# One ring of three two-bank PSUM buffers for the first layer and the attention

## The chip, the cores and the metric

The kernel runs on one core of a Trainium2 chip. The metric is device time in microseconds (us) of one launch; lower is better. The core has five engines that run their own instruction queues in order: TensorE (PE in the profile; its weight loads are listed apart as PEld), VectorE (DVE), ScalarE (ACT), GpSimd (POOL) and SyncE (SP), which here issues every DMA. Matmuls write into PSUM, of which this kernel uses eight banks of 512 fp32 columns in 128 partitions; DVE and ACT read it from there.

## The reference, cut to what matters

All data are float32 (the two weight matrices come as float64). Agent attention runs first, over two batches of 12480 tokens, 49 agents and 128 channels; its output goes through one dense layer pair with an ELU between.

```python
scale = 1.0 / np.sqrt(q.shape[-1])
def sm(a, b):
    s = scale * (a @ b.transpose(0, 2, 1))
    s = s - s.max(-1, keepdims=True)
    e = np.exp(s)
    return e / (e.sum(-1, keepdims=True) + 1e-09)
agent_v = sm(agents, k) @ v            # per batch: 49 x 128
x = (sm(q, agents) @ agent_v).reshape(B * S, D)
h = x @ w_in                           # 24960 x 2048
g = np.where(h > 0.0, h, np.exp(np.minimum(h, 0.0)) - 1.0)
out = g @ w_out                        # 24960 x 128
```

The kernel never forms x. It multiplies agent_v by w_in once per batch (49 x 2048, called A), and h is the query softmax times A.

## The kernel before, in words

**Tiling.** A block is 960 tokens (8 groups of 120); there are 13 blocks a batch, 26 in all. A block is worked in two halves of 480 tokens, each half in 8 steps, and a step covers 256 of the 2048 hidden columns. So the main loop has 26 x 2 x 8 = 416 steps, and a period of 16 steps is one block. High and low parts of fp32 numbers are kept apart (hi and lo, px and py for the two parts and two orders of the softmax rows), which is why a step has several matmuls for one product.

**A step s** is, in the order in which the loop at the end of the function writes it: `p1(s)`, six matmuls into a two-bank tile h (line 407); `p2(s - 4)`, eight matmuls of an earlier step into the output banks o0 and o1 (line 437), and after the eighth step of a half two DVE operations that add these into ob (lines 440, 441) and its DMA; `elu(s)`, Relu and Exp on ACT (413, 414) and the DVE operation that makes g (416); `split(s)`, the DVE cast hi (422) and the POOL subtraction lo (line 194, called through `rest`); and then whatever `at(s, ...)` has put into the table `pre` for this step. Nothing reorders this: the order is written by hand, each engine runs its own part of it in order, and semaphores follow from the tiles that are written and read.

**PSUM.** Pool ps_h has two h tiles of two banks each, used in turn; ps_o has o0 and o1; ps_a has two single banks, at0 and at1, that `attn_bank` hands out and `attn_free` takes back. An h tile is free again when g of its step has been computed.

**Attention work in the table.** Let EDGE be 3. For query block j the table holds, from step s0 = 16 (j - 1) + 3 on: scores of 960 tokens (`q_scores`, 8 matmuls, line 146), the maximum and its subtraction one step later (`q_max` 303, `q_sub` 314), `q_exp` (320), `q_sum` (323), `q_rz` (328, 331), `q_mul` (335), `q_hi` (189) and `q_lo` (194), and at s0 + 8 and s0 + 9 the two halves of `q_tr`: four transposes each (361), a copy into px (362), and two DMAs that make py by swapping px's row groups (365, 366). The scores' bank is held from `q_scores` to the last `q_lo`: the exponentials are kept in it. Batch 1's keys are scored in 13 rounds, two a period, in steps 8 to 104 (`k_round`, then `k_out` a step later: an ACT copy, line 154, and DVE maxima, lines 160 and 164); then four small calls spread the maximum (`k_max_*`). From step 116 on each round's scores are shifted (`e_sub`, 198), exponentiated (`e_exp`, 201) and multiplied with v (`ev1_pe`, line 207, four matmuls and two steps later four more). All 104 of these matmuls add up in one bank, which is held for the whole stretch; `ev1_out` copies it. Then `av_pe`, `av_out` and four times `A_pe`, `A_hi`, `A_lo` make A of batch 1.

**Before the loop** batch 0's keys and values are worked, and the weights are converted from float64 (lines 97 to 110), which goes on into the first steps of the loop. Two tiles of the h ring, `two` and `hk`, serve here too.

Of the kernel before, what the change touches and what calls it, by code (L numbers as in the profile page):

```python
# [22 lines left out]
def tile_agent_attention_moe(  # L23
# [34 lines left out]
    v_p = ctx.enter_context(tc.tile_pool(name="v", bufs=5))  # L58
    sm_p = ctx.enter_context(tc.tile_pool(name="sm", bufs=2))
    wc_p = ctx.enter_context(tc.tile_pool(name="wc", bufs=2))  # L60
    ps_h = ctx.enter_context(tc.tile_pool(name="ps_h", bufs=2, space=bass.MemoryType.PSUM))
    ps_o = ctx.enter_context(tc.tile_pool(name="ps_o", bufs=1, space=bass.MemoryType.PSUM))
    ps_a = ctx.enter_context(tc.tile_pool(name="ps_a", bufs=1, space=bass.MemoryType.PSUM))

    ag_sb = const.tile([C, B, NA], F32)
    ident = const.tile([128, 128], F32)
# [61 lines left out]
        nc.sync.dma_start(out=t, in_=vx[b, :, r * R:(r + 1) * R, :])  # L128
        v_t[b, r] = t

    idle = [0, 1]
    held = {}

    def attn_bank(dt=F32):
        i = idle.pop(0)
        ps = ps_a.tile([128, 512], dt, tag=f"at{i}", name=f"at{i}")
        held[id(ps)] = i
        return ps

    def attn_free(ps):  # L140
        if id(ps) in held:
            idle.append(held.pop(id(ps)))

    def scores_pe(ps, src, b, lo, hi):
        for j in range(lo, hi):
            nc.tensor.matmul(out=ps[:TP, j * NA:(j + 1) * NA], lhsT=src[:, j * TP:(j + 1) * TP], rhs=ag_sb[:, b, :], start=True, stop=True)  # L146
# [58 lines left out]
    def ev_pe(ps, b, r, lo, hi, rs):  # L205
        for j in range(lo, hi):
            nc.tensor.matmul(out=ps, lhsT=s_all[:, r, j:j + 2, :].rearrange("p t a -> p (t a)"), rhs=v_t[b, r][:, j, :], start=(r == rs[0] and j == 0), stop=(r == rs[-1] and j == R - 1))  # L207
        if hi == R:
            v_t.pop((b, r))
# [20 lines left out]
        else:  # L230
            nc.vector.scalar_tensor_tensor(out=av["sv"], in0=ps, scalar=f, in1=av["sv"], op0=ALU.mult, op1=ALU.add)

    def ev1_pe(r, lo, hi):
        if r == 0 and lo == 0:
            ev_ps[0] = attn_bank()
        ev_pe(ev_ps[0][:2 * NA, 0:VW], 1, r, lo, hi, range(NR))

    def ev1_out():
        ps = ev_ps.pop(0)
        attn_free(ps)  # L240
        av["sv"] = sm_p.tile([NA, VW], F32, tag="sv", name="sv")
        nc.vector.tensor_copy(out=av["sv"], in_=ps[:NA, 0:VW])

    def av_pe():
        ps = attn_bank()
# [57 lines left out]
        nc.vector.tensor_reduce(out=mx, in_=v, axis=AX.X, op=ALU.max)  # L303
        q_st["mx"] = mx

    def q_sub(keep=True):
        ps = q_st.pop("ps")
        v = ps[:TP, 0:R * NA].rearrange("p (t a) -> p t a", a=NA)
        if keep:
            e, q_st["z"], q_st["bank"] = v, ps[:TP, 400:400 + R], ps  # L310
        else:
            e = sm_p.tile([TP, R, NA], F32, tag="qe", name="qe", bufs=1)
            q_st["z"] = sm_p.tile([TP, R], F32, tag="z", name="z")
        nc.vector.tensor_tensor(out=e, in0=v, in1=q_st["mx"].unsqueeze(2).to_broadcast([TP, R, NA]), op=ALU.subtract)
        if not keep:
            attn_free(ps)
        q_st["e"] = e

    def q_exp():
        nc.scalar.activation(out=q_st["e"], in_=q_st["e"], func=ACTF.Exp, scale=scale)  # L320

    def q_sum():
        nc.vector.tensor_reduce(out=q_st["z"], in_=q_st["e"], axis=AX.X, op=ALU.add)

    def q_rz(half):
        z = q_st["z"]
        if half == 0:
            nc.vector.tensor_scalar(out=z, in0=z, scalar1=1e-9, scalar2=None, op0=ALU.add)
        else:
            q_st["z"] = sm_p.tile([TP, R], F32, tag="z", name="z")  # L330
            nc.vector.reciprocal(out=q_st["z"], in_=z)

    def q_mul(eng):
        e = q_st["e"]
        eng.tensor_tensor(out=e, in0=e, in1=q_st["z"].unsqueeze(2).to_broadcast([TP, R, NA]), op=ALU.mult)
# [4 lines left out]
    def q_hi(eng):  # L340
        for h, t in enumerate(halves(pp_hi)):
            cast_hi(eng, t, q_st["e"][:, h * (R // 2):(h + 1) * (R // 2), :])

    def q_lo(eng, lo=0, hi=R):
        for x in range(lo, hi, R // 2):
            h = x // (R // 2)
            rest(eng, halves(pp_lo)[h], q_st["e"][:, x:x + R // 2, :], halves(pp_hi)[h])
        if hi == R:
            attn_free(q_st.pop("bank", None))

    def q_tr(j, part):

        if part == 0:
            p_t[j] = []
        src = (pp_hi, pp_lo)[part]
        x = sm_p.tile([NA2, T], F32R, tag=f"px{part}", name=f"px{part}")
        y = sm_p.tile([NA2, T], F32R, tag=f"py{part}", name=f"py{part}")
        p_t[j].append((x, y))
        ps = attn_bank(F32R)
        for i in range(R // 2):  # L360
            nc.tensor.transpose(ps[:NA2, i * TP:(i + 1) * TP], src[:, i, :], ident_r[:TP, :TP])  # L361
        nc.vector.tensor_copy(out=x, in_=ps[:NA2, 0:T])
        attn_free(ps)
        a, b = [slice(r, r + NA) for r in ROWS]
        nc.sync.dma_start(out=y[a].bitcast(F32), in_=x[b].bitcast(F32))
        nc.sync.dma_start(out=y[b].bitcast(F32), in_=x[a].bitcast(F32))
# [31 lines left out]

    def p1(s):
        j, half, c = at_step(s)  # L400
        h = ps_h.tile([128, 2, 512], F32, tag="h", name="h")
        ah, al = A[j // NG, c]
        hi, lo = p_t[j]
        for i, (a, p) in enumerate([(ah, hi), (ah, lo), (al, hi)]):
            for u, r in enumerate(ROWS):
                x = slice(r, r + NA)
                nc.tensor.matmul(out=h[:, u, 0:T], lhsT=a[x, :], rhs=p[u ^ half][x, :], start=i == 0, stop=i == 2)  # L407
        h_t[s] = h[:, :, 0:T]
# [40 lines left out]
    def at(s, fn, *a):  # L449
        pre.setdefault(s, []).append((fn, a))  # L450

    with tc.manual_schedule():
        with tc.tile_pool(name="pro", bufs=5) as pro:
# [33 lines left out]
            two = ps_h.tile([128, 2, 512], F32, tag="h", name="h")  # L487
# [60 lines left out]
            def spread():  # L548
# [25 lines left out]
                ("e11", lambda: q_tr(0, 0), lambda: q_tr(0, 1)),  # L574
# [36 lines left out]
        for j in range(1, B * NG):  # L611
            s0 = (j - 1) * NM + EDGE
            if j + 1 < B * NG:
                at(s0 + 1, load_q, j + 1)
            if j > 1:
                at(s0, q_scores, j, 0, R)
                at(s0 + 1, q_max)
                at(s0 + 1, q_sub)
            at(s0 + 2, q_exp)
            at(s0 + 3, q_sum)  # L620
            at(s0 + 3, q_rz, 0)
            at(s0 + 4, q_rz, 1)
            at(s0 + 4, q_mul, dve)
            at(s0 + 5, q_hi, act)
            at(s0 + 6, q_lo, dve, 0, 4)
            at(s0 + 7, q_lo, dve, 4, 8)
            at(s0 + 8, q_tr, j, 0)
            at(s0 + 9, q_tr, j, 1)
        ks = {}
# [12 lines left out]
        KM = (3, 4, 6, 7)
        at(k_end + KM[0], lambda: k_max_t(mx_st["run"], attn_bank()))
        at(k_end + KM[1], k_max_d, 0)
        at(k_end + KM[2], lambda: k_max_b(attn_bank()))
        at(k_end + KM[3], k_max_c)
# [61 lines left out]
```

## Time and profile before

| | us |
|---|---|
| median of 3 runs | 1227.63 |
| lowest and highest | 1218.49, 1231.73 |
| the profiled execution | 1230.22 |
| its span, first to last instruction | 1228.4 |
| start of the first step of the loop | 70.4 |

Mean granted TensorE clock over the span: 0.966. A line of the timeline has the start in us from the span's start, the duration in us, the engine, the line, the operation, what it writes and reads, shapes and a count; in brackets the idle time of the engine before it and what ended that. A line of a group has busy time, the mean duration of one in ns, and the idle time before it. A line of a stretch has from:to, its length, then busy time of each engine with the number of instructions, the granted clock, the share of the DMA engines and GB/s.

### The profile page before, as it was taken

The page shows a single profiled execution, that of the slowest core. Times are in us where ns is not written, and L with a number is a line of the kernel's source. Part 1 is how long each engine was busy: PE and PEld are TensorE (multiplying, and loading weights), DVE is VectorE, ACT ScalarE, POOL GpSimd, SP SyncE. Part 2 cuts the span into 40 slices and gives each one's busy share as a digit, 9 for nine tenths or more (in the row PEclk, how much of TensorE's full clock was granted, in tenths as well). Part 3 has the DMA queues.
Part 4 walks back from the last instruction along what each step waited for, and adds up shares of the span by engine and source line. Part 5 has one row for each costly group of instructions (what it writes and reads, how often), then busy time and mean ns, then how long its engine had stood idle before and what let it go on. Part 6 is the DMA issues. An engine that isn't in the chain of part 4 may idle for free.

```text
span 1228.4 us, 21453 instructions
## 1 busy us (share of the span) xinstructions
PE 1166.6 (95%) x8184; PEld 815.3 (66%) x8184; DVE 883.5 (72%) x1353; ACT 881.2 (72%) x998; POOL 523.6 (43%) x443
## 2 busy tenths in 40 slices
PE   9877999999999999999999999999999999999998
PEld 9844666666666666667666566666666666666676
DVE  5564576676777676776767777778777777778775
ACT  3344676676777676776777778887878788787886
POOL 0123343344444343443444444544445444544454
PEclk9877899899999899999999999999999999999999
DMA  9940112112112113113001001101110101100000
GB/s 288 244 135 1 37 49 70 37 41 77 38 42 61 54 46 89 54 41 94 21 25 45 22 27 43 46 21 38 34 45 21 45 26 45 32 35 33 21 30 17
DMA packets 25709, 66.63 MB, mean 54 GB/s; under 512 B 3054, under 2 KB 14806, under 8 KB 25606
## 3 DMA queue, kind: packets, MB, share of 16 engines
q1 hardware_dynamic: 25606, 65.26, 17.4%
q8 instruction: 64, 1.05, 0.4%
q14 instruction: 39, 0.32, 0.1%
HBM read 42.68 MB, written 12.78 MB: 45 GB/s over the span
## 4 chain that ended last, share of the span: by engine, by line
PE 61%; DVE 20%; ACT 12%; issue 3%; DMA 3%; POOL 0%; DVEq 0%; SPq 0%; ACTq 0%; POOLq 0%
PE o L437 30%; PE h L407 18%; DVE g L416 11%; PE at L146 6%; ACT e L414 5%; ACT e L413 5%; PE at L207 2%; DVE hi L422 2%; PE at L361 2%; DMA v<-in_vx_dram 1%; PE h L207 1%; DVE mx L303 1%; DVE ob L441 1%; DVE ob L440 1%; PE at L262 1%
## 5 line engine op out<-in xcount | busy, mean ns | idle before, releaser
L194 POOL TENSOR_TENSOR lo<-g,hi 128x480 fp32r<-128x480 f32 x416 | 506.9, 1219 | 641.1 <-DVE hi L422 543.0
L416 DVE SCALAR_TENSOR_TENSOR g<-e,h 128x960 f32<-128x960 f32 x416 | 478.7, 1151 | 226.2 <-ACT e L414 215.6
L413 ACT ACTIVATE e<-h 128x960 f32<-128x960 f32 x416 | 403.0, 969 | 243.3 <-PE h L407 195.4
L414 ACT ACTIVATE e<-e 128x960 f32<-128x960 f32 x416 | 418.7, 1007 | 13.1
L437 PE MATMUL o<-g,w_f 64*128 64x480 f32 x1664 | 422.3, 574 | 0.0
L437 PE MATMUL o<-lo,w_hi 64*128 64x480 f32 x832 | 330.4, 766 | 0.0
L407 PE MATMUL h<-px,ahi 49*128 49x480 f32 x832 | 275.7, 411 | 19.6 <-DVE g L416 13.9
L407 PE MATMUL h<-py,ahi 49*128 49x480 f32 x832 | 275.7, 411 | 10.6 <-DVE g L416 7.2
L422 DVE CAST hi<-g 128x480 fp32r<-128x480 f32 x416 | 171.4, 412 | 57.6 <-PE o L437 3.8
L407 PEld LDWEIGHTS h<-px,ahi 49*128 49x128 f32 x832 | 135.2, 189 | 85.3 <-DVE g L416 56.5
L437 PE MATMUL o<-hi,w_lo 64*128 64x480 f32 x832 | 177.8, 388 | 13.9 <-POOL w_lo L194 8.2
L437 PEld LDWEIGHTS o<-g,w_f 64*128 64x128 f32 x1664 | 168.6, 189 | 24.0
L407 PEld LDWEIGHTS h<-py,ahi 49*128 49x128 f32 x832 | 135.1, 189 | 70.4 <-DVE g L416 48.9
L437 PE MATMUL o<-hi,w_hi 64*128 64x480 f32 x832 | 172.5, 385 | 0.0
L407 PE MATMUL h<-px,alo 49*128 49x480 f32 x416 | 159.6, 384 | 2.9 <-DVE alo L284 2.9
L407 PE MATMUL h<-py,alo 49*128 49x480 f32 x416 | 159.4, 383 | 0.1
L437 PEld LDWEIGHTS o<-lo,w_hi 64*128 64x128 f32 x832 | 89.0, 190 | 83.4 <-issue 79.7
L437 PEld LDWEIGHTS o<-hi,w_lo 64*128 64x128 f32 x832 | 87.0, 187 | 39.8 <-DVE ob L441 11.8
L437 PEld LDWEIGHTS o<-hi,w_hi 64*128 64x128 f32 x832 | 86.5, 190 | 11.0
L407 PEld LDWEIGHTS h<-px,alo 49*128 49x128 f32 x416 | 78.3, 188 | 11.1 <-DVE alo L284 4.6
L407 PEld LDWEIGHTS h<-py,alo 49*128 49x128 f32 x416 | 78.3, 188 | 7.1 <-DVE alo L284 1.3
L146 PEld LDWEIGHTS at<-ag_sb,q 128*120 128x120 f32 x400 | 43.9, 185 | 12.4 <-issue 12.4
(112 smaller groups left out, 719.0 us busy)
## 6 DMA issues: line engine op xcount, KB each, us to landing
v<-in_vx_dram SPq DMA_DIRECT2D x26, 483.8 KB
k<-in_kT_dram SPq DMA_DIRECT2D x26, 480.0 KB
q<-in_qT_dram SPq DMA_DIRECT2D x26, 480.0 KB
out_dram<-ob SPq DMA_DIRECT2D x52, 240.0 KB
py<-px SPq DMA_DIRECT2D x104, 91.9 KB
raw<-in_w_out_dram SPq DMA_DIRECT2D x4, 512.0 KB
raw<-in_w_in_dram SPq DMA_DIRECT2D x3, 512.0 KB
k<-in_w_in_dram SPq DMA_DIRECT2D x1, 512.0 KB
```

The source lines that it names most:

```text
L146: nc.tensor.matmul(out=ps[:TP, j * NA:(j + 1) * NA], lhsT=src[:, j * TP:(j + 1) * TP], rhs=ag_sb[:, b, :], start=True, stop=True)
L194: eng.tensor_tensor(out=out, in0=x, in1=hi.bitcast(F32), op=ALU.subtract)
L207: nc.tensor.matmul(out=ps, lhsT=s_all[:, r, j:j + 2, :].rearrange("p t a -> p (t a)"), rhs=v_t[b, r][:, j, :], start=(r == rs[0] and j == ...
L262: nc.tensor.matmul(out=av[b, lo][:NA2, 0:hi - lo], lhsT=av["t"], rhs=win_sb[:, lo:hi], start=True, stop=True)
L303: nc.vector.tensor_reduce(out=mx, in_=v, axis=AX.X, op=ALU.max)
L361: nc.tensor.transpose(ps[:NA2, i * TP:(i + 1) * TP], src[:, i, :], ident_r[:TP, :TP])
L407: nc.tensor.matmul(out=h[:, u, 0:T], lhsT=a[x, :], rhs=p[u ^ half][x, :], start=i == 0, stop=i == 2)
L413: nc.scalar.activation(out=e, in_=h, func=ACTF.Relu, scale=-1.0)
L414: nc.scalar.activation(out=e, in_=e, func=ACTF.Exp, scale=-1.0)
L416: nc.vector.scalar_tensor_tensor(out=g, in0=e, scalar=-1.0, in1=h, op0=ALU.add, op1=ALU.max)
L422: nc.vector.tensor_copy(out=hi_t[s], in_=g_t[s][:, 0, :])
L437: nc.tensor.matmul(out=o_t[u][:, 0:T], lhsT=w[x, c, :], rhs=v[x, :], start=first and i == 0, stop=last and i == len(jobs) - 1)
```

## The change

Pool ps_a goes, and ps_h has three tiles of two banks in place of two. In the loop, attention takes its PSUM from the same ring: `slot` gives the next two-bank tile, and `attn_bank` its first bank (in the prologue the two halves of a tile called `pair` stand for the two single banks). The h tiles and the attention tiles take turns in this ring, in the order of the program. With it go these moves:

- query scores are reduced and subtracted in the step of their matmuls, and the exponentials go to an SBUF tile `qe`; all later steps of the query softmax come one step earlier
- all eight transposes are in one step, into the two banks of one tile, with the two copies behind them
- a key round's copy and maxima are in the step of its scores, and the maximum's spreading follows at once
- each of the 13 rounds of agent values of batch 1 is its own group of eight matmuls in one step, and DVE adds it to a sum in SBUF
- `A_hi` and `A_lo` follow their `A_pe` in the same step.

```diff
-    ps_h = ctx.enter_context(tc.tile_pool(name="ps_h", bufs=2, space=bass.MemoryType.PSUM))
+    ps_h = ctx.enter_context(tc.tile_pool(name="ps_h", bufs=3, space=bass.MemoryType.PSUM))
     ps_o = ctx.enter_context(tc.tile_pool(name="ps_o", bufs=1, space=bass.MemoryType.PSUM))
-    ps_a = ctx.enter_context(tc.tile_pool(name="ps_a", bufs=1, space=bass.MemoryType.PSUM))
...
-    idle = [0, 1]
+    idle = []
     held = {}
 
-    def attn_bank(dt=F32):
-        i = idle.pop(0)
-        ps = ps_a.tile([128, 512], dt, tag=f"at{i}", name=f"at{i}")
-        held[id(ps)] = i
+    def slot(dt=F32):
+
+        return ps_h.tile([128, 2, 512], dt, tag="h", name="h")
+
+    def attn_bank():
+
+        if not idle:
+            return slot()[:, 0, :]
+        ps = idle.pop(0)
+        held[id(ps)] = ps
         return ps
...
+    def ev1(r):
+        ps = attn_bank()
+        ev_pe(ps[:2 * NA, 0:VW], 1, r, 0, R, (r,))
+        if r == 0:
+            av["sv"] = sm_p.tile([NA, VW], F32, tag="sv", name="sv")
+            nc.vector.tensor_copy(out=av["sv"], in_=ps[:NA, 0:VW])
+        else:
+            nc.vector.tensor_tensor(out=av["sv"], in0=av["sv"], in1=ps[:NA, 0:VW], op=ALU.add)
...
+    def q_tr(j, banks):
+
+        p_t[j] = []
+        for part, (src, ps) in enumerate(zip((pp_hi, pp_lo), banks)):
+            x = sm_p.tile([NA2, T], F32R, tag=f"px{part}", name=f"px{part}")
+            y = sm_p.tile([NA2, T], F32R, tag=f"py{part}", name=f"py{part}")
+            p_t[j].append((x, y))
+            for i in range(R // 2):
+                nc.tensor.transpose(ps[:NA2, i * TP:(i + 1) * TP], src[:, i, :], ident_r[:TP, :TP])
         a, b = [slice(r, r + NA) for r in ROWS]
-        nc.sync.dma_start(out=y[a].bitcast(F32), in_=x[b].bitcast(F32))
-        nc.sync.dma_start(out=y[b].bitcast(F32), in_=x[a].bitcast(F32))
+        for (x, y), ps in zip(p_t[j], banks):
+            nc.vector.tensor_copy(out=x, in_=ps[:NA2, 0:T])
+            nc.sync.dma_start(out=y[a].bitcast(F32), in_=x[b].bitcast(F32))
+            nc.sync.dma_start(out=y[b].bitcast(F32), in_=x[a].bitcast(F32))
+
+    def q_ring(j):
+        t = slot(F32R)
+        q_tr(j, [t[:, i, :] for i in range(2)])
...
             if j > 1:
                 at(s0, q_scores, j, 0, R)
-                at(s0 + 1, q_max)
-                at(s0 + 1, q_sub)
-            at(s0 + 2, q_exp)
...
+                at(s0, q_max)
+                at(s0, q_sub)
+            at(s0 + 1, q_exp)
+            at(s0 + 2, q_sum)
+            at(s0 + 2, q_rz, 0)
+            at(s0 + 3, q_rz, 1)
+            at(s0 + 3, q_mul, dve)
+            at(s0 + 4, q_hi, act)
+            at(s0 + 5, q_lo, dve, 0, 4)
+            at(s0 + 6, q_lo, dve, 4, 8)
+            at(s0 + 8, q_ring, j)
         def k_round(r):
-            ks[r] = attn_bank()
-            scores_pe(ks[r], k_t.pop((1, r)), 1, 0, R)
+            ps = attn_bank()
+            scores_pe(ps, k_t.pop((1, r)), 1, 0, R)
+            k_out(ps, r, r == 0)
...
-            for i in range(2):
-                at(s0 + 2 * i, ev1_pe, r, 4 * i, 4 * i + 4)
-        s0 += 6
-        at(s0, ev1_out)
+            at(s0, ev1, r)
         at(s0 + 3, av_pe)
-        at(s0 + 4, av_out)
+        at(s0 + 3, av_out)
         for c in range(4):
-            d = s0 + 7 + 4 * c
-            at(d, A_pe, 1, 512 * c, 512 * c + 512)
-            at(d + 2, A_hi, 1, 512 * c, 512 * c + 512)
-            at(d + 3, A_lo, 1, 512 * c, 512 * c + 512)
+            at(s0 + 6 + 4 * c, A_pe, 1, 512 * c, 512 * c + 512)
+            at(s0 + 6 + 4 * c, A_out, 1, 512 * c, 512 * c + 512)
```

More of the change, by code (lines that the diff above doesn't have):

```diff
@@ L129, in load_v @@
         v_t[b, r] = t
-    idle = [0, 1]
+    idle = []
     held = {}
-    def attn_bank(dt=F32):
-        i = idle.pop(0)
-        ps = ps_a.tile([128, 512], dt, tag=f"at{i}", name=f"at{i}")
-        held[id(ps)] = i
+    def slot(dt=F32):
[5 more added lines that the diff above has]
+        held[id(ps)] = ps
         return ps
     def attn_free(ps):
-        if id(ps) in held:
-            idle.append(held.pop(id(ps)))
+        if held.pop(id(ps), None) is not None:
+            idle.append(ps)
     def scores_pe(ps, src, b, lo, hi):
@@ L231, in ev0_add @@
             nc.vector.scalar_tensor_tensor(out=av["sv"], in0=ps, scalar=f, in1=av["sv"], op0=ALU.mult, op1=ALU.add)
[L233 to L242, printed above, removed]
+    def ev1(r):
[6 more added lines that the diff above has]
+            nc.vector.tensor_tensor(out=av["sv"], in0=av["sv"], in1=ps[:NA, 0:VW], op=ALU.add)
     def av_pe():
@@ L304, in q_max, with q_sub @@
         q_st["mx"] = mx
-    def q_sub(keep=True):
+    def q_sub():
         ps = q_st.pop("ps")
         v = ps[:TP, 0:R * NA].rearrange("p (t a) -> p t a", a=NA)
[L309 to L313, printed above, removed]
+        e = sm_p.tile([TP, R, NA], F32, tag="qe", name="qe", bufs=1)
         nc.vector.tensor_tensor(out=e, in0=v, in1=q_st["mx"].unsqueeze(2).to_broadcast([TP, R, NA]), op=ALU.subtract)
-        if not keep:
-            attn_free(ps)
+        attn_free(ps)
         q_st["e"] = e
@@ L322, in q_sum @@
     def q_sum():
+        q_st["z"] = sm_p.tile([TP, R], F32, tag="z", name="z")
         nc.vector.tensor_reduce(out=q_st["z"], in_=q_st["e"], axis=AX.X, op=ALU.add)
@@ L347, in q_lo @@
             rest(eng, halves(pp_lo)[h], q_st["e"][:, x:x + R // 2, :], halves(pp_hi)[h])
[L348 to L363, printed above, removed]
-        a, b = [slice(r, r + NA) for r in ROWS]
-        nc.sync.dma_start(out=y[a].bitcast(F32), in_=x[b].bitcast(F32))
-        nc.sync.dma_start(out=y[b].bitcast(F32), in_=x[a].bitcast(F32))
+    def q_tr(j, banks):
[6 more added lines that the diff above has]
+                nc.tensor.transpose(ps[:NA2, i * TP:(i + 1) * TP], src[:, i, :], ident_r[:TP, :TP])
+        a, b = [slice(r, r + NA) for r in ROWS]
+        for (x, y), ps in zip(p_t[j], banks):
[5 more added lines that the diff above has]
+        q_tr(j, [t[:, i, :] for i in range(2)])
     wr_t = {}
@@ L400, in p1 @@
         j, half, c = at_step(s)
-        h = ps_h.tile([128, 2, 512], F32, tag="h", name="h")
+        h = slot()
         ah, al = A[j // NG, c]
@@ L486, in tile_agent_attention_moe @@
             loads("k0 k1 k2 k3 i0 k4 k5 k6 k7")
-            two = ps_h.tile([128, 2, 512], F32, tag="h", name="h")
+            two = slot()
             ev_ps[0], ev_ps[1] = two[:2 * NA, 0, 0:VW], two[:2 * NA, 0, 256:256 + VW]
@@ L504, in tile_agent_attention_moe @@
                 dve.tensor_copy(out=dup[:, r:r + NA], in_=ident[:NA, 0:NA])
-            hk = ps_h.tile([128, 2, 512], F32, tag="h", name="h")
+            hk, pair = slot(), slot()
+            idle[:] = [pair[:, i, :] for i in range(2)]
             def sc(r):
@@ L536, in conv @@
                     x()
-            qq = [q_max, lambda: q_sub(False), q_exp, q_sum, lambda: q_rz(0), lambda: q_rz(1), lambda: q_mul(dve), lambda: q_hi(act), lambda: q_lo(dve)]
+            qq = [q_max, q_sub, q_exp, q_sum, lambda: q_rz(0), lambda: q_rz(1), lambda: q_mul(dve), lambda: q_hi(act), lambda: q_lo(dve)]
             def run(l, n=1):
@@ L573, in tile_agent_attention_moe @@
                 ("e10", lambda: ev0_add(1)),
-                ("e11", lambda: q_tr(0, 0), lambda: q_tr(0, 1)),
+                ("e11", lambda: q_tr(0, [x.bitcast(F32R) for x in idle])),
                 ("e12",),
@@ L598, in tile_agent_attention_moe @@
             q_max()
-            q_sub(False)
+            q_sub()
+            idle.clear()
         x_p = ctx.enter_context(tc.tile_pool(name="x", bufs=2))
@@ L616, in tile_agent_attention_moe @@
                 at(s0, q_scores, j, 0, R)
-                at(s0 + 1, q_max)
-                at(s0 + 1, q_sub)
-            at(s0 + 2, q_exp)
[L620 to L629, printed above, removed]
+                at(s0, q_max)
[9 more added lines that the diff above has]
+            at(s0 + 8, q_ring, j)
         def k_round(r):
-            ks[r] = attn_bank()
-            scores_pe(ks[r], k_t.pop((1, r)), 1, 0, R)
+            ps = attn_bank()
+            scores_pe(ps, k_t.pop((1, r)), 1, 0, R)
+            k_out(ps, r, r == 0)
         for r in range(NR):
@@ L637, in tile_agent_attention_moe @@
             at(s0, k_round, r)
-            at(s0 + 1, lambda r=r: k_out(ks.pop(r), r, r == 0))
             if r > 1:
@@ L641, in tile_agent_attention_moe @@
         k_end = s0 + 4
[L642 to L646, printed above, removed]
+        at(k_end, lambda: k_max_t(mx_st["run"], attn_bank()))
+        at(k_end, k_max_d, 0)
+        at(k_end + 2, lambda: k_max_b(attn_bank()))
+        at(k_end + 2, k_max_c)
         for r in range(NR):
```

## The prediction

> **What bounds the kernel now.** I read the page first, then the steps by stage, then single steps in the timeline.
>
> ```profile
> span 1228.4 us, 21453 instructions
> PE 1166.6 (95%) x8184; PEld 815.3 (66%) x8184; DVE 883.5 (72%) x1353; ACT 881.2 (72%) x998; POOL 523.6 (43%) x443
> PE 61%; DVE 20%; ACT 12%; issue 3%; DMA 3%; POOL 0%; DVEq 0%; SPq 0%; ACTq 0%; POOLq 0%
> ```
>
> PE looks full, but a third of the chain that ended last is DVE and ACT, so PE waits for them somewhere. The main loop has 416 steps; a step is six matmuls into h (L407), eight into o (L437), two activations (L413, L414) and the DVE operation that makes g (L416). The Relu of L413 occurs once a step, so its rows cut the loop into stages (length, ACT busy, count):
>
> ```profile
> 70.37:146.63 76.26, 15.53 (x16) 0.73 0.10 31
> 146.63:425.19 278.56, 92.96 (x96) 0.96 0.16 52
> 425.19:656.90 231.71, 77.35 (x80) 1.00 0.18 52
> 656.90:744.66 87.76, 31.05 (x32) 0.98 0.10 32
> 744.66:1181.69 437.03, 170.56 (x176) 1.00 0.11 34
> ```
>
> Call the last four A (k rounds of batch 1), B (agent values of batch 1), C, D (query attention alone). A step takes 2.90, 2.90, 2.74 and 2.48 us there. Two clean steps of D:
>
> ```profile
> 822.00 0.38 PE L407 MATMUL h<-py,ahi 49*128 49x480 f32 x1
> ...
> 822.66 0.38 PE L437 MATMUL o<-hi,w_lo 64*128 64x480 f32 x2
> ...
> 822.86 0.97 ACT L413 ACTIVATE e<-h 128x960 f32<-128x960 f32 x1
> ...
> 823.87 1.01 ACT L414 ACTIVATE e<-e 128x960 f32<-128x960 f32 x1
> ...
> 824.90 1.16 DVE L416 SCALAR_TENSOR_TENSOR g<-e,h 128x960 f32<-128x960 f32 x1 [0.42 <-ACT e L414]
> ...
> 826.23 0.38 PE L407 MATMUL h<-px,ahi 49*128 49x480 f32 x1
> ```
>
> From 822.00 to 826.23 are two steps: 2.11 us each. With two h buffers, step s+2 writes the buffer that g(s) frees. Here g ends at 826.06, and PE takes the buffer at 826.23: the loop closes with 0.17 us to spare. Whatever delays ACT or DVE by more than that stops PE, as here:
>
> ```profile
> 799.36 0.56 DVE L303 TENSOR_REDUCE mx<-at 120x8 f32<-120x392 f32 x1
> ...
> 799.96 0.57 DVE L314 TENSOR_TENSOR at<-at,mx 120x392 f32<-120x392 f32 x1
> ...
> 800.44 1.14 DVE L416 SCALAR_TENSOR_TENSOR g<-e,h 128x960 f32<-128x960 f32 x1
> ...
> 801.64 0.48 PE L407 MATMUL h<-px,ahi 49*128 49x480 f32 x1 [0.26 <-DVE g L416]
> ```
> ```profile
> 801.64:804.21 2.57, 2.39 (x18) 1.44 (x18) 1.56 (x2) 2.51 (x4) 1.22 (x1) 1.00 0.00 0
> ```
>
> Two softmax operations push g back, and PE starts h right after g. The step from 801.64 is 0.46 us too long, yet PE counts as busy for 2.39 of its 2.57 us. So I measure stalls by step length, not by busy time. The Trainium skill ("Perfetto Trace Analysis", Identifying the Most-Contended Engine) also calls matmul busy time a bad measure of headroom; these rows agree.
>
> **What PE must do for attention.** Pieces of attention matmuls, and the h matmuls that follow:
>
> ```profile
> 792.94 1.88 PE L146 MATMUL at<-ag_sb,q 128*120 128x49 f32 x16
> ...
> 794.75 0.48 PE L407 MATMUL h<-px,ahi 49*128 49x480 f32 x1
> ...
> 796.96 0.39 PE L407 MATMUL h<-px,ahi 49*128 49x480 f32 x1
> ```
> ```profile
> 813.76 0.61 PE L361 MATMUL at<-ident_r,pp_hi 120*113 120x120 f32 x4
> ...
> 814.30 0.49 PE L407 MATMUL h<-py,ahi 49*128 49x480 f32 x1
> ```
> ```profile
> 556.20 1.08 PE L207 MATMUL at<-v,s_all 120*98 120x129 f32 x8
> ```
>
> Scores of 960 tokens take 1.81 us, four transposes 0.54 (eight: I take 1.0), one round of agent values at most its 1.08. A step that follows a piece is 2.21 long, 0.1 more than a clean one. Floors, at 2.11 a step and 2.81 a query block (1.81 + 1.0):
> A: 96 steps 202.6, 6 query blocks 16.9, 11 k rounds 19.9: 239.4, so 39.2 us of stall.
> B: 168.8, 5 blocks 14.1, 13 rounds 14.0: 196.9, stall 34.8.
> C: 67.5 and 5.6: 73.1, stall 14.6, among it four A_pe matmuls, which are work and stay: 4 us (an estimate, each like a round's 1.08).
> D: 371.4 and 11 blocks 30.9: 402.3, stall 34.8.
> Together 123.4 us. The 76 us of the first 16 steps wait for the weights' conversion, which the diff leaves, and I cost them at nothing.
>
> **The change, part by part.** *Ring of three.* Where no piece intervenes, step s+3 waits for g(s): the 0.17 us becomes 0.17 + 2.11. A piece takes one place; in the two following steps the loop is two deep again, and the third waits for the piece's evacuation. The piece itself, which had banks of its own, now waits on PE for the g of two steps back, and the next h matmul is queued behind it; but that g ends 4.06 us after its step's start (826.06 - 822.00), and the piece comes at three steps, 6.3. What counts is whether the evacuations end in time.
>
> *Scores, q_max and q_sub in one step.* After the scores at 792.94 DVE waited for the next g:
>
> ```profile
> 795.70 0.41 DVE L422 CAST hi<-g 128x480 fp32r<-128x480 f32 x1
> ...
> 797.75 1.16 DVE L416 SCALAR_TENSOR_TENSOR g<-e,h 128x960 f32<-128x960 f32 x1 [1.64 <-ACT e L414]
> ```
>
> q_max and q_sub (0.56 + 0.57) fit into 1.64, so they cost nothing; the slot is free at about 797.3, and the third h after it comes only at 799.1. If they did not fit, g would slip as it did at 800.44. A k round's copy and maximum move likewise into the scores' own step: ACT waits there anyway for h, which comes after the scores. The copy stands ahead of the next Relu, so a late score would hold that; the row shows PE, not ACT, as the late one.
>
> *Lag.* A later q_exp or q_hi on ACT delays Relu, exp and g.
>
> ```profile
> L320 ACT ACTIVATE at<-at 120x392 f32<-120x392 f32 x24 | 11.6, 482 | 17.4 <-DVE at L314 17.4
> L189 ACT ACTIVATE pp_hi<-at 120x196 fp32r<-120x196 f32 x48 | 13.5, 333 | 12.6 <-DVE at L335 12.5
> ```
>
> ACT's own work is 0.97 + 1.01 = 1.98 of 2.11 us, so it makes up 0.13 a step. q_exp (0.48, step 4 of a period of 16) leaves 0.1 at step 7; q_hi (two of 0.33) makes it 0.77, and step 10 still has 0.4. Three buffers bear 2.28, so h does not wait. What is late next is the output: its two DVE operations (ob) stand in g's queue, and the next o matmul waits for them. Without cover and without lag it costs this:
>
> ```profile
> 1190.15 0.38 PE L407 MATMUL h<-px,ahi 49*128 49x480 f32 x1
> ...
> 1191.91 0.48 PE L437 MATMUL o<-hi,w_lo 64*128 64x480 f32 x1 [0.27 <-DVE ob L441]
> ...
> 1193.26 0.38 PE L407 MATMUL h<-px,ahi 49*128 49x480 f32 x1
> ```
>
> 3.11 - 2.11 = 1.0 us, twice a period. Scores cover the output of step 3:
>
> ```profile
> 790.73 0.38 PE L407 MATMUL h<-px,ahi 49*128 49x480 f32 x1
> ...
> 793.88 0.65 DVE L441 TENSOR_TENSOR ob<-ob,o 128x480 f32<-128x480 f32 x1
> ```
>
> ob is done 794.53 - 790.73 = 3.80 us after its step began. At step 11 eight transposes end the step at 2.11 + 1.0, and the first o matmul comes 0.66 later (822.66), at 3.77: just met without lag, 0.4 late with step 10's. Bounds 0 and 1.0 for each of 24 periods; 0.4 gives 9.6.
>
> *q_tr in one step.* Both banks come from one slot, so the second four transposes no longer wait a step. Its two px copies and four SP transfers follow one another:
>
> ```profile
> 817.59 0.74 SPq L365 DMA_DIRECT2D py<-px  x1
> ...
> 820.51 0.70 SPq L366 DMA_DIRECT2D py<-px  x1
> ```
>
> The h matmul at 826.23, a new period, needs them: the last was issued 5.7 us ahead. After the change ob ends at 3.8 of step 11, then come g (1.15), hi (0.41) and a px copy (an estimate, as ob's 0.65): 6.0, and three issues of 0.7 before the last, 8.2. The period turns at 3.1 + 2.6 + 3 x 2.11 = 12.0: 3.8 us ahead. I cannot see the landing. Between 0 and 0.5 us a period (0 to 12) I take 4 in all. Loads behind them on SP are due over ten steps later.
>
> *Agent values.* Eight matmuls in one step and a sum in SBUF for each of 13 rounds. The nearest sum out of PSUM:
>
> ```profile
> L231 DVE SCALAR_TENSOR_TENSOR sv<-o,f,sv x1: 345/345/345, 67.2 to 67.2; 49x129 f32<-49x129 f32 x1
> L198 DVE TENSOR_TENSOR s_all<-s_all,mb x26: 516/561/1316, 19.4 to 630.5; 120x392 f32<-120x392 f32 x26
> ```
>
> 13 x 0.345 = 4.5 us of DVE, spread over 13 steps with idle time like the 1.64 above. What B has besides is e_sub (L198, up to 1.32) in front of a g, with its exponential on ACT behind, in the stretch where a piece every four steps makes the loop two deep: bounds 0 and 13 x 1.32 = 17; I take 7, some 0.5 a round. Once the last transposes and av_pe fall into one step, and the next h has a ring of one: it waits for its own predecessor's g, which ends 4.06 after a step's start (826.06 - 822.00) where the next h would come at about 3.1, and ob stands in front: 2 us.
>
> *The rest.* k_max's calls and A_hi, A_lo move to earlier steps, and in the prologue one two-bank tile stands for the two single banks: the same operations, once each, nothing.
>
> **The sum.** Of 123.4 us there stay 7.9 after pieces (72 of them in A to D, 0.11 each), 9.6 (ob), 4 (transfers), 7 + 2 (B) and 4 (A_pe): 34.5. The gain is 88.9: the profiled execution's 1230.2 us becomes 1141. That execution lies 2.6 above the median of the runs, 1227.6, so I write **1140 us** for a median. The forecast's own range is 1118 (only 7.9 and 4 stay) to 1173 (ob, transfers and B at their upper bounds, 14 + 8 + 10 more).
>
> **Rivals.** *SBUF contention.* q_mul and q_lo now read two SBUF tensors while POOL works. e_sub does so and goes from 0.56 to 1.32. The same q_mul once ran on SBUF beside POOL:
>
> ```profile
> 111.47 0.57 DVE L335 TENSOR_TENSOR qe<-qe,z 120x392 f32<-120x392 f32 x1
> 111.48 1.62 POOL L194 TENSOR_TENSOR lo<-g,hi 128x480 fp32r<-128x480 f32 x1 [2.13 <-DVE z L331]
> ```
>
> There POOL paid, which has idle time. If DVE pays, 1.2 us a block over 24 blocks: 1169. The Trainium skill ("SBUF — State Buffer", Who interferes with whom) says such a DVE instruction contends with a GpSimd one that reads SBUF and that issue order decides who blocks; e_sub agrees. 0.10.
>
> *PE is full.* If the 95% were true work, only 1228.4 - 1166.6 = 61.8 us could go: 1168 at best. The 2.39 of 2.57 us speaks against. 0.07.
>
> *The ring gains only away from pieces.* If steps within two of a piece keep their stall, about half remains: 1185. 0.10.
>
> *Slower.* Every one of some 80 pieces (the 72 and the small ones) holds its slot until DVE, in order behind g and hi, has evacuated it, and the h matmul two or three steps later waits. The gain is gone at 89/80 = 1.1 us a piece; at 1.5 the kernel takes 1141 + 120 = 1261. For it: evacuations stand behind 1.57 us of g and hi. Against: two steps later is 4.2 us later. 0.05.
>
> *Nothing*: within 1% of 1227.6, about what a measurement tells from no change, if stalls move to waits of equal length. 0.05.
>
> The forecast itself has 0.63. The range 1118 to 1185 leaves out the last two cases and what little lies beyond the third's value. Faster by over 1%: 0.90; within: 0.05; slower: 0.05.
>
> **What would show it.** Stage D falls from 39.7 us a period to 37.4, A and B from 46.4 to about 41 and 42. Steps well away from a piece take 2.11 to 2.15. PE's waits for g almost vanish; those for ob stay. q_sub and q_max lie between hi and the next g. I am wrong if h waits for L303, L314, L160 or L362, if q_mul takes over 1 us, or if A and B keep over 44 us a period.

## The result, and the profile after

The changed kernel takes 1182.99 us (median; 1175.36 to 1186.57), the kernel before 1228.43 (1218.49 to 1231.73). The ratio is 0.963, 95% interval 0.956 to 0.969: 3.7% faster. The forecast was 1140 us, range 1118 to 1185. The sign and the stated range held; of 88.9 us forecast, about half came. The forecast's own range, 1118 to 1173, did not hold: the result lies in the stated one only because that takes in the times of the rivals.

The profiled execution of the changed kernel took 1186.57 us. Its page (span, busy times, the chain that ended last):

```profile
span 1184.8 us, 21530 instructions
PE 1145.1 (97%) x8184; PEld 884.5 (75%) x8184; DVE 900.9 (76%) x1365; ACT 878.6 (74%) x998; POOL 536.4 (45%) x443
PE 68%; DVE 18%; ACT 9%; issue 3%; POOL 0%; DVEq 0%; DMA 0%; SPq 0%; POOLq 0%; ACTq 0%
```

DVE and ACT still have 27% of the chain, where they had 32% before, so time is still lost to them somewhere. The same stages as in the prediction, cut again at the Relu, now L412 (from:to, length, ACT busy and count, granted clock, DMA share, GB/s):

```profile
83.47:155.26 71.79, 15.52 (x16) 0.71 0.08 29
155.26:403.92 248.66, 92.98 (x96) 1.00 0.18 56
403.92:627.72 223.80, 77.08 (x80) 0.99 0.19 55
627.72:708.24 80.52, 30.93 (x32) 0.98 0.11 35
708.24:1137.87 429.63, 170.09 (x176) 0.98 0.11 35
```

Against these stand the prediction's terms for each stage (its floor plus what it let stay; C with its 4 us for A_pe). The last column is a kernel of the experiments below.

| | before | forecast | after | after − forecast | e3_noz |
|---|---|---|---|---|---|
| start of the loop | 70.4 | 70.4 | 83.5 | +13.1 | 71.7 |
| first 16 steps | 76.3 | 76.3 | 71.8 | −4.5 | 72.1 |
| A, 96 steps | 278.6 | 245.3 | 248.7 | +3.4 | 245.4 |
| B, 80 steps | 231.7 | 211.2 | 223.8 | +12.6 | 221.1 |
| C, 32 steps | 87.8 | 78.6 | 80.5 | +1.9 | 78.0 |
| D, 176 steps | 437.0 | 410.9 | 429.6 | +18.7 | 413.0 |
| behind D | 46.7 | 46.7 | 46.9 | +0.2 | 46.8 |

The fifth column adds up to 45.4 us, the whole of 1186.6 − 1141. Three places carry it: the time before the loop, B and D. I take them in this order.

**Before the loop.** Two rounds of batch 0's key scores in the timeline of the changed kernel (in brackets the idle time before and what ended it):

```profile
8.99 2.90 PE L151 MATMUL h<-ag_sb,k 128*120 128x49 f32 x16 [0.90 <-ACT s_all L167]
...
24.07 3.44 PE L151 MATMUL h<-ag_sb,k 128*120 128x49 f32 x16 [0.70 <-ACT s_all L167]
```

In these two, the round goes into the second half of `pair` and waits there for ACT's copy of the round before, which reads the first half. These are PE's only gaps between 8 and 50 us, 1.6 us together, yet the loop starts 13 us later. Stretches of 10 us from there (length; busy time and count of PE, PEld, DVE, ACT, POOL; granted clock; DMA share; GB/s):

```profile
10.00:20.00 10.00, 10.00 (x51) 10.00 (x51) 2.31 (x6) 1.18 (x3) 0.00 (x0) 0.50 1.03 349
20.00:30.00 10.00, 9.30 (x47) 9.01 (x47) 2.47 (x8) 2.43 (x5) 0.00 (x0) 0.50 1.01 273
30.00:40.00 10.00, 10.00 (x50) 9.82 (x49) 4.40 (x10) 2.53 (x5) 1.27 (x1) 0.50 1.00 235
40.00:50.00 10.00, 10.00 (x50) 10.00 (x51) 3.41 (x9) 2.66 (x5) 0.00 (x0) 0.50 0.99 257
```

For 40 us TensorE is granted half its clock, while it counts as 93 to 100% busy: the same matmuls take longer. A busy share can't show that; the clock column does.

**B.** One round of agent values in its step:

```profile
446.91 0.38 PE L406 MATMUL h<-px,ahi 49*128 49x480 f32 x1
...
449.11 2.02 PE L212 MATMUL h<-v,s_all 120*98 120x129 f32 x16
...
451.05 0.48 PE L406 MATMUL h<-px,ahi 49*128 49x480 f32 x1
```

The step is 451.05 − 446.91 = 4.14 us, 2.03 over a clean one. The records count each of these fp32 matmuls twice: a round of eight matmuls is x16. The row of before that I read as a round, 1.08 us x8, was half of one.

**D.** Part of one period. I leave out what runs on time:

```profile
764.16 0.56 DVE L322 TENSOR_REDUCE z<-qe 120x8 f32<-120x392 f32 x1
764.39 1.22 POOL L199 TENSOR_TENSOR lo<-g,hi 128x480 fp32r<-128x480 f32 x1 [1.09 <-DVE hi L421]
...
764.75 0.88 DVE L327 TENSOR_SCALAR z<-z 120x8 f32<-120x8 f32 x1
...
765.54 1.14 DVE L415 SCALAR_TENSOR_TENSOR g<-e,h 128x960 f32<-128x960 f32 x1
...
767.37 0.57 DVE L334 TENSOR_TENSOR qe<-qe,z 120x392 f32<-120x392 f32 x1
...
767.97 0.63 ACT L194 ACTIVATE pp_hi<-qe 120x196 fp32r<-120x196 f32 x2 [1.42 <-DVE qe L334]
...
775.54 0.48 PE L406 MATMUL h<-py,ahi 49*128 49x480 f32 x1 [0.16 <-DVE g L415]
...
776.78 0.48 PE L436 MATMUL o<-hi,w_lo 64*128 64x480 f32 x1 [0.32 <-DVE ob L439]
...
777.54 0.73 PE L436 MATMUL o<-hi,w_lo 64*128 64x480 f32 x1 [0.28 <-DVE ob L440]
```

L327 adds 1e-9 to eight numbers a partition, and takes 0.88 us. Its group over the whole execution (busy us, mean ns, idle before), in the kernel before, in PSUM, and after, in SBUF:

```profile
L328 DVE TENSOR_SCALAR at<-at 120x8 f32<-120x8 f32 x24 | 4.2, 174 | 0.8
```
```profile
L327 DVE TENSOR_SCALAR z<-z 120x8 f32<-120x8 f32 x26 | 21.4, 823 | 0.9
```

Above it starts 0.36 us after POOL's lo and ends with it (764.75 + 0.88 = 765.63, 764.39 + 1.22 = 765.61). Then g is late, then q_mul, and ACT, which has q_hi next in its queue, waits 1.42 us. ACT catches up 0.2 a step (its next Relus come 1.90 apart), so at the transposes, three steps later, g and ob are still late and PE waits. In some periods the waits cost more: the same step 12 twice, in two neighbouring periods (stretch, length, the five engines as above, granted clock, DMA share, GB/s):

```profile
775.43:779.98 4.55, 3.84 (x16) 2.77 (x17) 4.17 (x8) 2.75 (x3) 2.03 (x3) 0.74 0.15 56
815.60:818.82 3.22, 2.64 (x16) 1.81 (x17) 2.88 (x6) 2.75 (x3) 1.26 (x2) 1.00 0.13 51
```

Where the clock falls in it, the period takes 40.1 to 40.3 us, elsewhere 38.4 to 38.5. Four of D's eleven periods fall so; the other seven have waits of about the same length at this place and keep the clock.

### The profile page after: what moved, and what is told of

The parts are those of the page before. It is cut to its first block, busy times and chain, and to the rows that moved or that the text cites. A ratio compares the mean times of both kernels' runs of the same rounds, so it can differ in the third digit from the quotient of the medians.

```text
span 1184.8 us, 21530 instructions
## 1 busy us (share of the span) xinstructions
PE 1145.1 (97%) x8184; PEld 884.5 (75%) x8184; DVE 900.9 (76%) x1365; ACT 878.6 (74%) x998; POOL 536.4 (45%) x443
## 4 chain that ended last, share of the span: by engine, by line
PE 68%; DVE 18%; ACT 9%; issue 3%; POOL 0%; DVEq 0%; DMA 0%; SPq 0%; POOLq 0%; ACTq 0%
PE o L436 39%; PE h L406 17%; DVE g L415 9%; PE h L151 7%; ACT e L412 4%; ACT e L413 3%; PE h L212 3%; DVE hi L421 2%; DVE ob L440 1%; DVE ob L439 1%; PE o L151 1%; ACT pp_hi L194 1%; DVE pp_lo L199 1%; DVE qe L334 1%; PE h L265 1%
## 5 line engine op out<-in xcount | busy, mean ns | idle before, releaser
L412 ACT ACTIVATE e<-h 128x960 f32<-128x960 f32 x416 | 402.2, 967 | 165.3 <-PE h L406 141.3
L436 PE MATMUL o<-g,w_f 64*128 64x480 f32 x1664 | 442.3, 572 | 0.0
L436 PE MATMUL o<-lo,w_hi 64*128 64x480 f32 x832 | 350.7, 765 | 0.0
L436 PE MATMUL o<-hi,w_lo 64*128 64x480 f32 x832 | 200.3, 389 | 17.7 <-POOL w_lo L199 8.3
L436 PEld LDWEIGHTS o<-g,w_f 64*128 64x128 f32 x1664 | 188.0, 189 | 23.7
L436 PE MATMUL o<-hi,w_hi 64*128 64x480 f32 x832 | 194.0, 386 | 0.0
L406 PEld LDWEIGHTS h<-px,ahi 49*128 49x128 f32 x832 | 151.8, 190 | 45.6 <-issue 25.8
L436 PEld LDWEIGHTS o<-lo,w_hi 64*128 64x128 f32 x832 | 107.0, 189 | 64.9 <-issue 55.8
L436 PEld LDWEIGHTS o<-hi,w_lo 64*128 64x128 f32 x832 | 105.4, 187 | 44.0 <-DVE ob L440 13.4
L436 PEld LDWEIGHTS o<-hi,w_hi 64*128 64x128 f32 x832 | 105.3, 190 | 10.3
L406 PEld LDWEIGHTS h<-py,alo 49*128 49x128 f32 x416 | 78.6, 189 | 6.0 <-DVE alo L287 0.8
L151 PEld LDWEIGHTS h<-ag_sb,q 128*120 128x120 f32 x416 | 45.7, 184 | 12.4 <-DVE g L415 11.9
```

What stands on the lines that cost most here:

```text
L412: nc.scalar.activation(out=e, in_=h, func=ACTF.Relu, scale=-1.0)
L436: nc.tensor.matmul(out=o_t[u][:, 0:T], lhsT=w[x, c, :], rhs=v[x, :], start=first and i == 0, stop=last and i == len(jobs) - 1)
```

## The experiments

They ask three things: what delays the loop's start, what the third buffer is worth against the moved steps, and whether the addition's wait beside POOL is the loss in D. The kernel before, run beside them, took 1226.39, 1226.04 and 1221.47 us in the three groups; a ratio is to the one beside it.

**The two kernels again.**

> The changed kernel once more. If its late loop start (83.5 us against 70.4 us before) comes from the two halves of one PSUM tile being serialised in the prologue, the loop starts again at 80 to 86 us, with the same waits of key scores for ACT's copies. If it was the clock's chance, the start moves towards 70 us in some run. From the start of the loop to the end it takes 1095 to 1105 us either way.

> The kernel before once more, to see how firm the start of its loop is. Serialised halves as the cause: 68 to 73 us. Chance of the clock as the cause: anywhere between 68 and 86 us.

After: 1181.96 us, loop from 80.43, a period 41.44 in A, 44.75 in B, 39.16 in D. Before: 1222.73 us, loop from 69.80, periods 46.16, 46.34, 39.73. What stands above is not one execution's luck. In this second execution of the changed kernel PE waits 0.90 and 0.97 us for ACT's copies, and the granted clock is 0.50 from 18 to 52 us, where it was so from 10 to 50 before; the loop starts 3 us earlier.

**Banks of their own in the prologue.** `e1_pro` gives the two single banks tiles of their own, in a pool that is closed before the loop; the ring's third tile opens then.

```diff
-        with tc.tile_pool(name="pro", bufs=5) as pro:
+        with tc.tile_pool(name="pro", bufs=5) as pro, tc.tile_pool(name="ps_p", bufs=1, space=PSUM) as ps_p:
...
-            hk, pair = slot(), slot()
-            idle[:] = [pair[:, i, :] for i in range(2)]
+            hk = slot()
+            idle[:] = [0, 1]
```

> The changed kernel, but the prologue's two attention banks are tiles of their own, as in the kernel before; they become the third tile of the ring only when the loop starts. If the serialised halves delay the prologue, the loop starts at about 70 us, the granted clock in the first 50 us is well above 0.50 most of the time, and the kernel is about 13 us faster than the changed one (1170 us). If the delay is the clock's chance, the loop starts at 70 or at 83 us, no matter which kernel. Loop itself unchanged.

1172.38 us (1170.35 to 1177.05), ratio 0.958 [0.953, 0.963]. The loop starts at 73.1 instead of 83.5; D stays at 39.19 a period. Over the first five stretches of 10 us the granted clock is 1.00, 1.00, 0.81, 0.68 and 1.00. In all the kernels here whose prologue has banks of its own, the profiled start lies between 65.6 and 74.0; in the two executions of the changed kernel it is 83.5 and 80.4. So `pair`, read and written as one buffer, costs the time before the loop, and nothing behind it. The size is less firm than the cause: 10 us by the medians, 6.5 by the two ratios (0.963 and 0.958).

**Warm-up matmuls in the waits.** `e3_warm` is the changed kernel with four warm-up matmuls instead of one ahead of each of the first seven key scores; `pair` is left, and the warm-up fills most of the waits for it.

```diff
-                    busy(1)
+                    busy(4)
```

> The changed kernel with three more warm-up matmuls ahead of each of the first seven key scores, while TensorE waits there for ACT's copies. If the low granted clock (0.50 from 10 to 50 us) is the price of the serialised prologue, the clock stays near 1.0 and the loop starts at 72 to 75 us instead of 83.5. If the waits themselves are the price, the start stays at 80 us or later.

A single execution: 1170.07 us, and the loop starts at 71.96. The stretches that answer to those above:

```profile
10.00:20.00 10.00, 9.94 (x92) 9.75 (x91) 3.25 (x9) 1.80 (x4) 0.00 (x0) 1.00 1.02 345
20.00:30.00 10.00, 9.65 (x87) 9.42 (x87) 6.54 (x15) 3.83 (x9) 1.26 (x1) 1.00 1.02 270
30.00:40.00 10.00, 10.00 (x94) 9.80 (x92) 7.65 (x17) 4.63 (x11) 1.27 (x1) 1.00 0.99 241
40.00:50.00 10.00, 10.00 (x95) 10.00 (x95) 6.36 (x16) 4.34 (x10) 1.27 (x1) 1.00 0.98 251
```

More matmuls, and the start comes 11.5 us earlier, with `pair` as it was: in this execution the low clock is the price, not the 1.6 us of waits. Whether it is the shorter pauses or the added matmuls that keep the clock up, this run doesn't tell. The Trainium skill ("TensorE: Matmul & The Clock Gate", What's actually happening) gives back the full clock after a window of about 3.4 us of sustained matmuls. The changed kernel doesn't show that: PE has no gap from 8.99 to 23.37 us, and stays at 0.50.

**The moves without the third buffer.** `e_moves` has all moved steps, but two h tiles and two single attention banks, as the kernel before (here they are taken strictly in turn).

```diff
-    ps_h = ctx.enter_context(tc.tile_pool(name="ps_h", bufs=3, space=PSUM))
+    ps_h = ctx.enter_context(tc.tile_pool(name="ps_h", bufs=2, space=PSUM))
+    ps_a = ctx.enter_context(tc.tile_pool(name="ps_a", bufs=1, space=PSUM))
...
-            return slot()[:, 0, :]
+        return ps_a.tile([128, 512], dt, tag=f"at{i}", name=f"at{i}")
```

> The moves without the ring: all attention work stands in the same steps as in the changed kernel, with the softmax in SBUF, but there are two h tiles and two separate attention banks, as before. If the third h tile is what brings the gain, steps 4 to 10 of a period without keys stay above 2.11 us wherever softmax work stands, a period of the last stage takes 39 us or more, and the kernel takes 1200 to 1235 us. If the moves bring the gain, it takes 1165 to 1190 us.

1182.51 us (1181.41 to 1191.03), ratio 0.968 [0.961, 0.974]. Its attention banks are two tiles in the prologue too (the loop starts at 65.6), so it is compared with `e1_pro`: 10 us slower. Its stages A and D:

```profile
139.57:392.44 252.87, 92.97 (x96) 1.00 0.17 55
...
703.30:1132.83 429.53, 170.22 (x176) 1.00 0.11 35
```

With two buffers A falls from 278.6 to 252.9, and D is what it is with three. The moves alone bring 44 of the 54 us that `e1_pro` gains (1226.39 − 1182.51 and 1226.39 − 1172.38), some 4 of them by the earlier start (65.6 against 69.8). The time is in the second of the ranges expected, while D's period of 39.05 is what was expected of the first. This is against my main reason, the loop of two buffers.

**Without the addition.** `e2_noz` and `e3_noz` are one kernel: `e1_pro` without the addition of 1e-9.

```diff
-        if half == 0:
-            nc.vector.tensor_scalar(out=z, in0=z, scalar1=1e-9, scalar2=None, op0=ALU.add)
-        else:
+        if half == 1:
```

> The kernel with the prologue's own banks, without the addition of 1e-9 to the softmax sums (left out: it takes 0.88 us beside POOL, where it took 0.17 us in PSUM before; the sums are over 1, so nothing is lost). If that addition makes the lag, g of its step comes 0.7 us earlier, ACT's wait for q_mul falls from 1.4 to about 0.6 us a block, the step of the output after the transposes shortens, and a period of the last stage falls from 39.2 to about 38 us. If ACT is simply full, the period stays at 38.4 to 40.

> Prologue banks of their own and no addition of 1e-9 to z (that part of the computation is left out: only the reciprocal of z is taken). If the wait of the addition beside POOL is what delays the queries, the whole kernel takes 1147 us (1142 to 1153), a period of the last stage 37.6 us and its step 11 about 3.2. If the single look at this edit was a lucky one, it comes out at 1160 to 1172.

`e2_noz`, a single execution: 1147.37 us. `e3_noz`, four: 1147.7 us (1144.14 to 1149.87), ratio 0.936 [0.929, 0.943]. The additions of eight numbers a partition, of which 24 took 0.88 us in the changed kernel's loop, are worth some 25 us (1172.38 − 1147.7; by the two ratios 26). The same place in its timeline, and stage D:

```profile
743.26 0.55 DVE L324 TENSOR_REDUCE z<-qe 120x8 f32<-120x392 f32 x1
...
745.57 0.57 DVE L334 TENSOR_TENSOR qe<-qe,z 120x392 f32<-120x392 f32 x1
...
746.17 0.62 ACT L196 ACTIVATE pp_hi<-qe 120x196 fp32r<-120x196 f32 x2 [0.51 <-DVE qe L334]
```
```profile
688.26:1101.30 413.04, 170.07 (x176) 1.00 0.11 36
```

ACT waits 0.51 us where it waited 1.42, step 12 takes 2.5 to 2.6 us, and the clock stays at 1.00 over D. The last column of the table above shows the forecast's A, C and D within 2.1 us of this kernel's.

**The third buffer once the lag is gone.** `e3_two` is `e_moves` without the addition.

> Two buffers for the first layer and two separate attention banks as before, with the moved steps, and no addition of 1e-9 (left out as in e3_noz). If the third buffer is worth what the prediction gave to it, the two-buffer loop shows once the lag is gone: 1165 to 1180 us, 38.2 to 38.6 us a period in the last stage. If the order of the steps alone decides, it is within 8 us of e3_noz, 1147 to 1155, and the last stage takes 37.6 a period.

1163.8 us (1162.45 to 1167.89), ratio 0.951 [0.945, 0.957]; A 247.32, B 225.62, C 79.49, D 419.57. It falls between the two cases expected, close to the first (D takes 38.1 a period). Against `e3_noz`, the third buffer is worth 16.1 us, of the 73.8 that `e3_noz` is below the kernel before. Their profiled executions are 18.0 us apart: 6.5 in D, 4.5 in B, 1.9 in A, 1.5 in C and 5.3 in the first 16 steps, while `e3_two` starts its loop 1.7 earlier. With the addition kept, `e_moves` against `e1_pro`, it is 10.1 us. The lists of waits (engine, line, waited for, us in total, times, longest) of before, the changed kernel, `e_moves` and `e3_two`, in this order:

```profile
PEld h L407 <- DVE g L416: 105.4, 205, 1.6
```
```profile
PEld h L406 <- DVE g L415: 10.4, 37, 0.6
```
```profile
PEld h L401 <- DVE g L410: 113.9, 246, 1.5
```
```profile
PEld h L399 <- DVE g L408: 93.3, 246, 0.9
```

The third buffer removes this wait, as I had said. But `e_moves` has more of it than the kernel before and is 44 us shorter, and `e3_two` pays 16 us for 93. A wait in such a list is not a price. These lines are of the weight loads alone (PEld); the same lists give 21.1, 4.8, 18.6 and 3.6 us for the h matmuls' own waits for g. In D of `e3_two` most of the seven steps behind the scores take 2.1 to 2.3 us (one takes 2.67), where the ring of three has 2.11. The ring gives 0.2 of that back at the scores, whose step takes 4.2 instead of 4.0.

**The addition one step later.** `e3_zlate` is `e1_pro` with the addition directly ahead of the reciprocal, before POOL's lo begins.

```diff
-            at(s0 + 2, q_rz, 0)
+            at(s0 + 3, q_rz, 0)
             at(s0 + 3, q_rz, 1)
```

> The addition of 1e-9 is kept, but stands one step later, directly ahead of the reciprocal and before POOL's lo part has begun. If it is slow because POOL works beside it, it takes 0.16 to 0.30 us instead of 0.88, a period of the last stage falls to 37.6 to 38.2 us, and the kernel takes 1147 to 1158 us. If the operand in SBUF is what makes it slow, it stays at about 0.88 and the time at 1168 to 1176. Third, if POOL's lo then lies beside the multiplication of the queries, that takes over 1 us instead of 0.57 and the time stays above 1165.

1182.41 us (1177.52 to 1182.96), ratio 0.965 [0.958, 0.971]. Against `e1_pro` that is no gain: 10 us slower by the medians, 9 by the ratios, whose intervals overlap. It is the third of the cases expected.

```profile
756.30 0.17 DVE L329 TENSOR_SCALAR z<-z 120x8 f32<-120x8 f32 x1
...
756.53 1.20 POOL L201 TENSOR_TENSOR lo<-g,hi 128x480 fp32r<-128x480 f32 x1 [0.86 <-DVE z L329]
756.74 1.42 DVE L336 TENSOR_TENSOR qe<-qe,z 120x392 f32<-120x392 f32 x1
...
758.19 0.63 ACT L196 ACTIVATE pp_hi<-qe 120x196 fp32r<-120x196 f32 x2 [1.56 <-DVE qe L336]
```

The same addition on the same SBUF operand takes 0.17 us ahead of POOL. Now q_mul starts 0.21 us behind POOL's lo and takes 1.42 instead of 0.57. In the changed kernel both started at 767.37, and there it was lo that took longer, 1.66 instead of 1.2. So the one that starts second pays, and where both start together it is lo.

**Later products.** `e2_hi` is `e1_pro` with q_hi one step later, so that ACT needn't wait for q_mul, and both parts of q_lo in the step after; `e2_both` has this and no addition; `e2_two` has both edits on two buffers (the addition is left out in it too).

```diff
-            at(s0 + 4, q_hi, act)
-            at(s0 + 5, q_lo, dve, 0, 4)
-            at(s0 + 6, q_lo, dve, 4, 8)
+            at(s0 + 5, q_hi, act)
+            at(s0 + 6, q_lo, dve, 0, 8)
```

> The kernel with the prologue's own banks, q_hi one step later and q_lo in one step behind it. If ACT's wait for q_mul makes the lag, that wait is gone, no Relu stands behind it, and a period of the last stage falls from 39.2 to 37.5 to 38 us. If the lag comes from ACT being full, the period stays above 38.4. Should the transposes now wait for q_lo, their step lengthens by up to 0.4 us.

> Both of these edits together with the prologue's own banks. If the lag theory holds, the two outputs a period are covered, no period has the clock dip, a period of the last stage takes 37.0 to 37.6 us, the loop falls from 1102 to about 1077 us, and the kernel takes about 1148 us. If ACT is full in any case, 1165 us or more.

> Both edits, but with two h tiles and two attention banks. If the third h tile is worth more once the lag is gone, this kernel takes 1165 to 1180 us, its last stage 38 us or more a period, with steps of 2.2 to 2.9 us behind softmax work, and the ring of three is 15 us or more ahead. If the order of the work alone decides, it comes within 8 us of the ring of three.

`e2_hi`: 1187.04 us in a single execution, no gain. `e2_both`: 1172.85 us (1167.02 to 1177.35), ratio 0.957 [0.951, 0.963]; it gives back all that leaving out the addition had brought. `e2_two`: 1185.77 us (1183.26 to 1187.43), ratio 0.968 [0.964, 0.972]. All three missed what was expected, and one row stands in all three timelines; in that of `e2_both`:

```profile
762.41 1.65 DVE L201 TENSOR_TENSOR pp_lo<-qe,pp_hi 120x196 fp32r<-120x196 f32 x2
...
763.98 1.14 DVE L415 SCALAR_TENSOR_TENSOR g<-e,h 128x960 f32<-128x960 f32 x1
764.06 0.47 PEld L356 LDWEIGHTS h<-ident_r,pp_hi 120*113 120x113 f32 x4 [0.52 <-DVE pp_lo L201]
```

ACT no longer waits ahead of q_hi, but q_lo's two subtractions, 0.36 us each in the changed kernel, now take 1.65 together while POOL's lo runs, directly ahead of g and of the transposes (1.65 in `e2_hi` and 1.66 to 1.67 in `e2_two`). The wait has only changed its place. That it is the whole of the three losses was not tried.

## Why the prediction was right, and where it was wrong

**"SBUF contention"** (the rival, 0.10, 1169 us). DVE did pay, and the size was near: 1.2 us a block over 24 blocks was 28.8 us, and the addition costs some 25. That the sizes are so near is luck, for the operation was another. I priced q_mul and q_lo, which in the changed kernel take their 0.57 and 0.36, and passed over the addition (174 ns in PSUM before); moved to SBUF with the rest, it stands behind POOL's lo. The Trainium skill ("SBUF — State Buffer", Who interferes with whom) does list `tensor_scalar` among the operations that can contend with GpSimd, in a mode that uses both ports, and says that whoever issues second is then blocked for the whole of the other's instruction. No run here shows that mode, but the order agrees: the addition ends 0.02 us behind lo (764.75 + 0.88 against 764.39 + 1.22), and q_mul in `e3_zlate` 0.43 behind it (756.74 + 1.42 against 756.53 + 1.20), 0.14 to 0.15 us short of a full wait with their own 0.17 and 0.57 after it. I had cited the section for q_mul and q_lo alone.

**"Lag": "q_hi makes it 0.77, and step 10 still has 0.4."** The walk was right, its start was not: with ACT's wait of 1.42 ahead of q_hi more is left at step 10, and ob and h wait at step 12. D: 39.1 a period instead of 37.4. Of the 18.7 us, (38.4 − 37.4) × 11 = 11 is this wait and about 4 × 1.8 = 7 the clock that falls behind it. Without the addition D takes 37.55, with the wait for ob forecast at 0.4 still there: step 12 lasts 2.5 to 2.6 us, 2.11 + 0.4.

**"One round of agent values at most its 1.08."** Mis-sized: 2.03 as a whole round. Thirteen times the difference of 0.95 is 12.4 us, and B came out 12.6 late. That these two agree so well is partly luck: without the addition B takes 221.1, so 2.7 us of it are the addition's, and my other terms there, the 7 and 2 for e_sub and the ring of one among them, were about as much too high. No run separates them. The kernel before paid the same matmuls; I had only counted work as stall that could go.

**"One two-bank tile stands for the two single banks: the same operations, once each, nothing."** This step failed: 13.1 us in the profiled execution, 10 in the medians against `e1_pro`. The operations were the same; the buffer was not. I costed instructions, and asked neither who shares the tile nor what a wait does to the clock.

**"Ring of three."** Right in what it does: steps away from a piece take 2.10 to 2.13 where the clock holds, the weight loads' waits for g fall from 105 to 10 us, and no h waits for q_sub or q_max. (For a k round's maximum its loads wait ten times, 2.1 us in all, and for a px copy h waits once, 1.0 us.) Wrong in what it is worth: 10 us by `e1_pro` and `e_moves`, 16.1 without the addition, by `e3_noz` and `e3_two`. The moves bring the rest of the gain. The floors were right but for B's rounds (`e3_noz`), but I gave the third buffer what belongs to the order: 0.17 us to spare is nearly enough where little is put ahead of g. Which of the moves brings how much was not tried.

**"PE is full"** (1168) is refuted by `e3_noz`, 1147.7 us with the same matmuls. **"The ring gains only away from pieces"** (1185) lies near the time by chance: steps after a piece take 2.22, as in the forecast. **"Slower"**: its 1.1 us a piece shows in one step only, the one after the transposes (3.22, once a period in D), and there it is mostly the addition's: without it that step takes 2.5 to 2.6. Of what I had named as proof against me, B at 44.8 us a period came.

## What to carry to other kernels

Before a small operation is moved into SBUF, ask what POOL does at that moment: beside it, 0.17 us became the rest of POOL's instruction, and where the next on that queue feeds the critical loop, such a wait can cost more than its own length (24 waits of 0.71 us, 17 in all, cost 25). Price a buffer by a loop with and without it, not by the waits that name it. And where two users share a tile, look at the granted clock, not only at the waits: two pauses under a microsecond came with half of it for 40 us.

## What the hardware showed that I had not expected

- An addition on 120x8 numbers took 0.17 us alone and 0.88 beside POOL, and moving it by one step moved the wait to the next two-input operation (0.57 to 1.42).
- The granted clock was 0.50 from 10 to 50 us, with pauses of 0.90 us just ahead and 0.70 us in it, and did not come back in 14 us without a pause, nor in most of the 26 behind the second. In a single execution with a few more matmuls in those pauses it stayed at 1.00 over this stretch. A pause is not needed for a fall: in the kernel before it was 0.50 from 21 to 24 us, with no pause over 0.12 us since the first matmul.
- In D the clock fell after waits of 0.2 to 0.3 us at three places of one step (0.74 over that step), in four of eleven periods. The Trainium skill ("TensorE: Matmul & The Clock Gate", What's actually happening) puts the fall after an idle window of about 3.4 us; these rows show it after far shorter waits. The other seven periods have such waits and no fall, so why it takes only some of them stays open.
